# A linear-attention and gated-MLP kernel on one core: a new order of the work, five instead of eight unread products at the start, and three small inputs in fewer packets

## The chip, the cores and the metric

The kernel runs on one core of a Trainium2 chip. The core has a matrix engine (TensorE, PE in the profile, with PEld for its weight loads), three engines for elementwise work (VectorE, DVE; ScalarE, ACT; GpSimd, POOL) and SyncE (SP), which here only issues transfers (DMA). Each engine runs its own instructions strictly in the order in which the program lists them, and waits by semaphores for what another engine or a transfer has to deliver. The metric is the time of one execution on the device in microseconds (us), the median over runs.

## The reference, cut to what matters

Four batches of four heads, sequence 1088, head dimension 32. Attention without softmax: each key and query is turned into 64 products of two 8-wide sketches. Then a gated MLP whose gate mixes along the sequence with a 1088 x 1088 matrix.

```python
def phi(x):
    a = np.einsum('rd,bhsd->bhsr', S1, x)
    b = np.einsum('rd,bhsd->bhsr', S2, x)
    return np.einsum('bhsi,bhsj->bhsij', a, b).reshape(*x.shape[:-1], r * r)
q_p, k_p = (phi(q), phi(k))
kv = np.einsum('bhsf,bhsd->bhfd', k_p, v)
z = np.sum(k_p, axis=2)
num = np.einsum('bhsf,bhfd->bhsd', q_p, kv)
den = np.einsum('bhsf,bhf->bhs', q_p, z)[..., None] + 1e-06
x = num / den                                # heads side by side: (4, 1088, 128)
...
h = np.maximum(x @ w_in, 0.0)                # (4, 1088, 1024)
u, v = (h[..., :d_ff // 2], h[..., d_ff // 2:])
v_n = (v - mu) / np.sqrt(var + 1e-06)        # mean and variance over the last axis
v_s = np.einsum('ts,bsd->btd', w_spatial, v_n) + b_spatial[None, :, None]
return ((u * v_s) @ w_out).astype(np.float32)
```

Some inputs (`S1`, `S2`, `w_in`, `w_out`) arrive as 64-bit floats, and the core turns them into 32-bit ones.

## The kernel before, in words

**Precision.** Large matrix products are made of three: every operand is split into a high half (rounded to the type that TensorE takes at full rate, `F32R`) and a low half, what is left. `high x high`, `high x low` and `low x high` are added up in one bank. So each product needs a cast on ScalarE (the high half) and a subtraction on VectorE or GpSimd (the low half). The spatial weights' halves are `wTh` and `wTl`, those of the normalised v are `vh` and `vl`.

**Stages.** For batch 0 (`attention0`), everything starts at once: the sketch matrices `sk` are loaded and turned from 64 bits to 32 in seven VectorE steps (`from_f64`, L459 to L470). TensorE projects keys and then queries by them in three groups (`project`, L559), ScalarE copies one factor (L564), VectorE multiplies the two into features (L567), TensorE sums keys against values (L606) into `kv`, and VectorE spreads `kv` to the block form `kd0` with a mask (L632). Query features are turned by TensorE with an identity (L655), multiplied with `kd0` (L669), divided on VectorE (L673 to L676), turned again (L683) and split into the halves `xh`, `xl` of x (L687, L688). The second half of the hidden layer, v, is made of 512-column products (L394 to L396), rectified on ScalarE (L771), and normalised with VectorE's statistics (L773 to L800) on VectorE (L809) or ScalarE (L812). Batch 0's v is split per block of 128 rows: L877 on ScalarE, L880 on VectorE (or GpSimd).

`main` then goes over blocks of 128 hidden features (d, four of them) and of output columns (c, three of them): per block nine products groups over the sequence (`spatial`: L940, L942 with the high half of the weights, L949 and L951 with the low half, the last with the bias as two extra rows), the first half of the hidden layer (`hidden`, L932 rectifies it), the gate (L977, then split by L474 and L404), and the output product (`out_mm`, L394 to L396 into a bank `po`). In batch 0 the first column block is done for all four d at once, first all products with the weights' high half, then with the low half. The attention of batch b+1 (`attention`) is woven into batch b's `main`; there the quotient is an elementwise reciprocal of 384 columns on VectorE (L747) and a product (L748), between the sums on TensorE and the 512-column products.

**Loads.** SP issues all transfers in one order, and at most eight are on their way. The first column block of the spatial weights comes in nine slices (`wt00` to `wt80`) into eight buffers (`pl`); a buffer is free again when both halves of its slice are made. The bias goes through a split and back by two transfers into rows of `wTl` (L536).

**What sets the order.** `Order.schedule` is a planner that runs when the program is built. Every operation has a cost written beside it, and a due time: TensorE's work in `main` has due times from `T_MAIN` and `PACE`, the others get theirs backwards from what uses them, shifted by the table `LEADS`. The planner keeps a clock per engine and repeatedly takes, of what could start first (within `SLACK`), the operation with the earliest due time. `FIRST` names loads that go ahead of the others. `AFTER` keeps batch 1's loads behind 35 us of the planner's clock; the built program has no such clock, only the order. Buffers come from pools with a fixed number of tiles, so the order also sets when an operation gets its buffer.

**Unread products.** At the very start TensorE does `N_WARM` products of zeros (L417), and where the planner sees TensorE without work for long enough in the first 50 us it puts further ones in (`fill`, L421; one for each `FILL` ns of the gap). Nobody reads them; they keep TensorE busy. In the profile each such product is two records.

## Time and profile before

| | |
|---|---|
| median of 3 runs (lowest to highest) | 335.91 us (334.52 to 336.27) |
| the profiled execution: its time, its span | 336.3 us, 334.5 us |
| busy in the span: PE, DVE, ACT, POOL | 326.8, 204.3, 157.2, 57.6 us |
| busy share of the 16 transfer engines, 5 to 10 and 10 to 15 us | 0.97, 0.96 |
| HBM read, written | 13.78 MB, 2.23 MB |

The span runs from the first to the last instruction. A row of the order of time gives start and length in us, engine, source line, operation, the tile written and the tiles read, their sizes, and the number of instructions in the row; in brackets stands the idle time just before it and what ended that idle time. Matrix products are pipelined and their ends are modelled, so the lengths of neighbouring rows overlap, and starts are the better measure. Tile names leave out buffer numbers.

### The profile page before, as it was taken

To read this page: it belongs to the slowest core of one execution; us is meant where nothing else is said; L and a number is where in the kernel's file an instruction comes from. 1 tells how busy PE (TensorE), PEld (TensorE's weight loads), DVE (VectorE), ACT (ScalarE), POOL (GpSimd) and SP (SyncE) were. 2 spreads that over 40 slices of the span, in tenths; PEclk is the share of its full clock that TensorE was granted. 3 is DMA by queue.
4 is the path that set the end of the run, shared out by engine and by line. 5 is a ranking of instruction groups with operands and counts; after the bars stand their busy time and mean duration, and the time that the engine had idled before them with its cause. 6 is when DMAs were issued, how large, how long until landed. Compare 5 with 4: busy or idle time off the path is not lost.

```text
span 334.5 us, 6021 instructions
## 1 busy us (share of the span) xinstructions
PE 326.8 (98%) x2308; PEld 314.6 (94%) x2308; DVE 204.3 (61%) x451; ACT 157.2 (47%) x366; POOL 57.6 (17%) x68
## 2 busy tenths in 40 slices
PE   8999999999999999999999999999999999999995
PEld 8977988999999999999999999999999999999994
DVE  3999999253899976679378566728783142121222
ACT  2599675434566762565445625445452242121212
POOL 1000112772423143420032316020000000000000
PEclk9999999999999999999999999999999999999999
DMA  7932267677210266401004173000000001000001
GB/s 225 314 118 69 52 174 222 139 140 164 81 50 21 51 117 153 116 6 43 2 20 77 65 135 62 2 0 0 3 0 2 22 3 44 0 2 0 0 2 67
DMA packets 18196, 23.09 MB, mean 69 GB/s; under 512 B 3064, under 2 KB 17912, under 8 KB 18168
## 3 DMA queue, kind: packets, MB, share of 16 engines
q1 hardware_dynamic: 18168, 22.71, 26.9%
q8 instruction: 18, 0.29, 0.4%
q14 instruction: 10, 0.08, 0.1%
HBM read 13.78 MB, written 2.23 MB: 48 GB/s over the span
## 4 chain that ended last, share of the span: by engine, by line
PE 82%; DVE 7%; DMA 4%; ACT 3%; SPq 1%; issue 1%; DVEq 0%; ACTq 0%
PE sp L940 20%; PE sp L942 17%; PE sp L949 17%; PE sd L394 3%; PE sd L395 3%; PE sd L396 3%; PE po L395 2%; PE pu L394 2%; PE po L394 2%; PE po L396 2%; PE sp L951 2%; PE pu L396 2%; PE pu L395 2%; PE sd L606 2%; DVE wTl L524 2%; DMA v<-in_vA 2%
## 5 line engine op out<-in xcount | busy, mean ns | idle before, releaser
L940 PE MATMUL sp<-wTh,vh 128*128 128x362 f32 (+4 forms) x414 | 135.4, 327 | 0.0
L942 PE MATMUL sp<-wTh,vl 128*128 128x362 f32 (+4 forms) x368 | 119.9, 326 | 0.6 <-DVE vl L880 0.6
L949 PE MATMUL sp<-wTl,vh 128*128 128x362 f32 (+4 forms) x368 | 117.6, 325 | 0.0
L940 PEld LDWEIGHTS sp<-wTh,vh 128*128 128x128 f32 x414 | 77.9, 188 | 1.4 <-ACT vh L877 0.2
L942 PEld LDWEIGHTS sp<-wTh,vl 128*128 128x128 f32 x368 | 69.2, 188 | 1.7 <-DVE vl L880 1.0
L949 PEld LDWEIGHTS sp<-wTl,vh 128*128 128x128 f32 x368 | 69.2, 188 | 0.2
L977 DVE TENSOR_TENSOR u<-sp,u 128x362 f32<-128x362 f32 (+3 forms) x36 | 18.2, 505 | 32.3 <-PE sp L951 27.6
L474 ACT CAST g<-u 128x362 fp32r<-128x362 f32 (+3 forms) x35 | 16.8, 481 | 30.4 <-DVE u L977 30.3
L747 DVE RECIPROCAL c<-c 128x384 f32<-128x384 f32 (+1 forms) x9 | 21.8, 2418 | 14.2 <-ACT c L745 11.5
L773 DVE BATCH_NORM_STATS2 st<-vt 128x6 f32<-128x512 f32 x36 | 24.2, 685 | 6.9 <-ACT vt L771 6.7
L771 ACT ACTIVATE vt<-sd 128x512 f32<-128x512 f32 x36 | 21.3, 600 | 13.1 <-PE sd L396 12.6
L977 DVE TENSOR_TENSOR kp<-sp,kp 128x424 f32<-128x424 f32 x10 | 6.0, 597 | 34.1 <-PE sp L951 34.1
L404 DVE TENSOR_TENSOR g<-u,g 128x362 fp32r<-128x362 f32 (+3 forms) x35 | 20.3, 581 | 8.6 <-ACT g L474 8.1
L716 POOL TENSOR_TENSOR pl<-pl,pl 128x384 f32<-128x384 f32 (+1 forms) x18 | 18.3, 1018 | 35.6 <-DMA pl<-abT 34.3
L407 POOL TENSOR_TENSOR r<-pl,r 128x384 fp32r<-128x384 f32 (+1 forms) x18 | 18.0, 1008 | 37.0 <-ACT r L474 36.9
L407 POOL TENSOR_TENSOR r<-c,r 128x384 fp32r<-128x384 f32 (+1 forms) x9 | 8.9, 993 | 86.9 <-ACT r L474 76.3
L849 ACT CAST vh<-vt 128x384 fp32r<-128x384 f32 x36 | 17.9, 512 | 11.4 <-DVE vt L809 9.0
L932 ACT ACTIVATE u<-pu 128x362 f32<-128x362 f32 (+3 forms) x36 | 16.4, 455 | 14.3 <-PE pu L396 14.3
L851 DVE TENSOR_TENSOR vl<-vt,vh 128x384 fp32r<-128x384 f32 (+1 forms) x36 | 19.4, 549 | 4.7 <-ACT vh L849 4.4
L394 PE MATMUL pu<-xh,wih 128*128 128x362 f32 (+4 forms) x48 | 16.0, 334 | 0.6 <-ACT kp L932 0.6
L809 DVE TENSOR_SCALAR vt<-vt,mv,sm 128x512 f32<-128x512 f32 x32 | 15.8, 537 | 0.0
L396 PE MATMUL pu<-xh,wil 128*128 128x362 f32 (+4 forms) x48 | 15.7, 327 | 0.0
(169 smaller groups left out, 546.7 us busy)
## 6 DMA issues: line engine op xcount, KB each, us to landing
pl<-in_wT SPq DMA_DIRECT2D x18, 166.0 KB, 2.6
v<-in_vA SPq DMA_DIRECT2D x12, 198.0 KB, 2.7
kt<-in_kT SPq DMA_DIRECT2D x12, 192.0 KB, 3.5
pl<-abT SPq DMA_DIRECT2D x12, 192.0 KB, 3.8
pl<-in_wT SPq DMA_DIRECT2D x9, 212.0 KB, 5.9
c<-in_qT SPq DMA_DIRECT2D x9, 192.0 KB, 2.6
pl<-abT SPq DMA_DIRECT2D x24, 72.0 KB, 2.5
pl<-abT SPq DMA_DIRECT2D x6, 160.0 KB, 4.0
```

The source lines that it names most:

```text
L394: nc.tensor.matmul(o, ah, bh, start=start, stop=False)
L395: nc.tensor.matmul(o, ah, bl, start=False, stop=False)
L396: nc.tensor.matmul(o, al, bh, start=False, stop=stop)
L404: return lambda: nc.vector.tensor_tensor(out=o(), in0=a(), in1=bb(), op=ALU.subtract)
L407: return lambda: nc.gpsimd.tensor_tensor(out=o(), in0=a(), in1=bb(), op=ALU.subtract)
L747: op("DVE", 135 + 6.3 * n, lambda x32=x32, n=n: nc.vector.reciprocal(out=x32[:, :n], in_=x32[:, :n]), w=[x32])
L771: op("ACT", c_act(512, True), lambda pv=pv, t=t: nc.scalar.activation(vt[:, t], pv.ap, AF.Relu), r=[pv], w=[(vt, t)])
L773: op("DVE", 690, lambda stats=stats, t=t: nc.vector.bn_stats(out=stats.ap, in_=vt[:, t]), r=[(vt, t)], w=[stats])
L940: nc.tensor.matmul(sp[:, :cw], vh[:, kt], wTh[:, kt, cs], start=(kt == 0), stop=False)
L942: nc.tensor.matmul(sp[:, :cw], vl[:, kt], wTh[:, kt, cs], start=False, stop=False)
L949: nc.tensor.matmul(sp[:, :cw], vh[:, kt], wTl[:, kt, cs], start=False, stop=False)
L977: op("DVE", c_dve(cw), lambda: nc.vector.tensor_tensor(out=u.ap, in0=sp[:, :cw], in1=u.ap, op=ALU.mult), r=[sp], w=[u], lead=LEAD[1])
```

## The change

It does six things.

1. `N_WARM` goes from 8 to 5.
2. The planner multiplies TensorE's costs by `COLD` = 1.25 before 6.8 us of its clock and counts one fill for each 460 ns of a gap there instead of 224. The unread products' own cost goes from 420 to 379 ns.
3. The planner's model of a load changes: a later landing of 1.05 to 1.95 us after issue, and a rate of 0.19 KB/ns before and 0.33 after 7.4 us of its clock, in place of 0.38 with one stop of 1.9 us.
4. The mask (128 rows of 24 bytes) becomes six more columns of the identity, so one transfer brings both; its readers read these columns.
5. The bias is laid out as 17 rows of 64 numbers instead of 68 rows of 16, in its load and in the two transfers into `wTl`, and its tiles come from the pools `abT` and `r`.
6. All tables of the planner are new (`T_MAIN`, `PACE`, `STRETCH`, `FIRST`, `LEADS`, `LEAD`, `SLACK`), so the order of everything is new. `FIRST` names four loads of the second and third column block.

```diff
-N_WARM = 8
+N_WARM = 5
...
-T_MAIN = (36.0, 126.0, 244.0, 299.0)
-PACE = (1.305, 0.8, 1.056, 1.506)
-STRETCH = 1.85
+T_MAIN = (26.0, 113.0, 216.0, 300.0)
+PACE = (1.043, 0.959, 1.6, 1.236)
+STRETCH = 3.08
...
-FIRST = ('wt22', 'wt11', 'wt02', 'qt02', 'wt01')
+FIRST = ('wt01', 'wt42', 'wt21', 'wt22')
...
-LEADS = {'W0': 19500, 'W0.0': -3000, 'W0.1': 18800,
...
+LEADS = {'W0': 4700, 'W0.0': -2000, 'W0.1': -10400,
...
-LEAD = (6500, 3700)
+LEAD = (8600, 700)
...
-SLACK = {'PE': 32, 'ACT': 56, 'DVE': 106, 'POOL': 890, 'SP': 84}
+SLACK = {'PE': 0, 'ACT': 0, 'DVE': 80, 'POOL': 1348, 'SP': 388}
 FILL, FILL_TO, FILL_SPARE = 224, 50.0, 150
+
+COLD_TO, FILL_COLD, COLD = 6800, 460, 1.25
...
-                n = int((s - free[e] - FILL_SPARE) // FILL)
+                n = int((s - free[e] - FILL_SPARE) // (FILL if s > COLD_TO else FILL_COLD))
...
+                cost *= COLD if s < COLD_TO else 1
...
-                dma = max(dma, s + cost + 1950) + o.kb / (0.38 if o.kb > 0 else -0.12)
-
-                if dma > 5000 and not slow:
-                    slow, dma = True, dma + 1900
+
+                late = 1950 if o.kb <= 0 else 1050 if s < 6000 else 1400
+                dma = max(dma, s + cost + late)
+                dma += o.kb / (-0.12 if o.kb <= 0 else 0.19 if dma < 7400 else 0.33)
...
-            kw["due"] = FIRST.index(t.name) - 1e4
+            kw["due"] = FIRST.index(t.name) * 1e5 - 1e8
...
-        op("PE", 420, f4=True, fn=lambda: nc.tensor.matmul(wps[:, :P], z9.ap, z9.ap, start=True, stop=True), r=[z9], w=[wps], due=0)
+        op("PE", 379, f4=True, fn=lambda: nc.tensor.matmul(wps[:, :P], z9.ap, z9.ap, start=True, stop=True), r=[z9], w=[wps], due=0)
...
-    ident = tl(None, "ident_sb", [P, P])
-    load(ident, lambda: ident.ap, idn, 64)
-
-    mask = tl(None, "mask_sb", [P, 6])
-    load(mask, lambda: mask.ap, msk, 2)
+
+
+    ident = tl(None, "ident_sb", [P, P + 6])
+    load(ident, lambda: ident.ap, idn, 70)
...
-        b32 = tl(None, "b32", [68, 16])
-        load(b32, lambda: b32.ap, bsp, 4)
-        bh, bl = tl(None, "bh", [68, 16], F32R), tl(None, "bl", [68, 16], F32R)
-        split(lambda: bh.ap, lambda: bl.ap, lambda: b32.ap, 16, [b32], [bh], [bl])
+        b32 = tl("abT", "b32", [P, 64])
+        load(b32, lambda: b32[:17], bsp, 4)
+        bh, bl = tl("r", "bh", [P, 64], F32R), tl("r", "bl", [P, 64], F32R)
+        split(lambda: bh[:17], lambda: bl[:17], lambda: b32[:17], 64, [b32], [bh], [bl])
...
-            in1=mask[:, 2:].unsqueeze(2).broadcast_to([P, 4, D + 1]), op=ALU.mult,
-        ), r=[kv, mask], w=[kd0])
+            in1=ident[:, P + 2:].unsqueeze(2).broadcast_to([P, 4, D + 1]), op=ALU.mult,
+        ), r=[kv, ident], w=[kd0])
```

Three places show how the order moves. Line numbers of the changed kernel are two or three higher for the same operation. First, TensorE's first instructions: L417 (now L420) and L421 (now L424) are unread, `sk,kt` is a projection of keys and `sk,c` of queries, `v,kp` the sums of keys and values, `ident_sb,kp` a turn of query features. Before:

```order
L417 MATMUL sd_76<-z_67 128x128 x8
L421 MATMUL po_113<-z_67 128x64 x3
L559 MATMUL sd_117<-sk,kt 64x2x32 x6
L559 MATMUL sd_76<-sk,kt 64x2x32 x6
L421 MATMUL po_113<-z_67 128x64 x4
L559 MATMUL sd_117<-sk,kt 64x2x32 x6
L421 MATMUL po_113<-z_67 128x64 x4
L606 MATMUL pu_162<-v,kp_132 64x66 x12
L559 MATMUL sd_76<-sk,c_95 64x2x32 x6
L606 MATMUL pu_162<-v,kp_138 64x66 x12
L606 MATMUL pu_162<-v,kp_151 64x66 x12
L559 MATMUL sd_117<-sk,c_136 64x2x32 x6
```

And now:

```order
L420 MATMUL sd_76<-z_67 128x128 x5
L424 MATMUL po_108<-z_67 128x64 x3
L561 MATMUL sd_112<-sk,kt 64x2x32 x6
L561 MATMUL sd_76<-sk,kt 64x2x32 x6
L424 MATMUL po_108<-z_67 128x64 x3
L561 MATMUL sd_112<-sk,kt 64x2x32 x6
L608 MATMUL pu_148<-v,kp_131 64x66 x12
L561 MATMUL sd_76<-sk,c_88 64x2x32 x6
L424 MATMUL po_108<-z_67 128x64 x4
L608 MATMUL pu_148<-v,kp_137 64x66 x12
L657 MATMUL po_108<-ident_sb,kp_131 128x128 x3
L657 MATMUL po_204<-ident_sb,kp_131 128x128 x3
```

Three products of the first kind and five fills are gone up to the first sums, the first query's turn comes ahead of the third group of sums, and the second and third queries' projections follow those sums. Further on five fills (four before) stand ahead of the first turn of x, and none ahead of the first L669.

Second, VectorE from the first features on: L567 (now L569) are features, of keys three times and then of queries, L460 to L470 (now L463 to L473) the steps that turn `w_in` (`vt`, then `v`) to 32 bits, L676 (now L678) the first quotient. Before:

```order
L567 TENSOR_TENSOR kp_151<-ka_130,sd_117 128x768
L460 TENSOR_SCALAR vt_155<-vt_155 128x512
L462 TENSOR_SCALAR vt_155<-vt_155 128x512
L463 SCALAR_TENSOR_TENSOR vt_155<-vt_89,vt_155 128x512
L567 TENSOR_TENSOR kp_132<-ka_134,sd_76 128x768
L468 TENSOR_SCALAR vt_155<-vt_155 128x512
L632 TENSOR_TENSOR kd_232<-pu_162,mask_sb 128x132
L469 SCALAR_TENSOR_TENSOR vt_155<-vt_89,vt_155 128x512
L567 TENSOR_TENSOR kp_138<-ka_130,sd_117 128x768
L470 TENSOR_TENSOR vt_155<-vt_155 128x512
L567 TENSOR_TENSOR kp_151<-ka_134,sd_76 128x768
L673 TENSOR_SCALAR sm_283<-sp_258 128x12
```

And now, from the third key features to the third query features:

```order
L569 TENSOR_TENSOR kp_163<-ka_129,sd_112 128x768
L569 TENSOR_TENSOR kp_131<-ka_133,sd_76 128x768
L463 TENSOR_SCALAR vt_175<-vt_175 128x512
...
L471 TENSOR_SCALAR vt_175<-vt_175 128x512
L634 TENSOR_TENSOR kd_237<-pu_148,ident_sb 128x132
L472 SCALAR_TENSOR_TENSOR vt_175<-vt_94,vt_175 128x512
L569 TENSOR_TENSOR kp_137<-ka_129,sd_112 128x768
L473 TENSOR_TENSOR vt_175<-vt_175 128x512
L675 TENSOR_SCALAR sm_272<-sp_249 128x12
...
L678 TENSOR_TENSOR c_119<-sp_249,sm_272 128x384
L407 TENSOR_TENSOR wil<-vt_175,wih 128x512
L466 SCALAR_TENSOR_TENSOR v<-kt,v 128x512
L569 TENSOR_TENSOR kp_131<-ka_133,sd_76 128x768
```

The first query features move ahead of the conversion, and the third ones from ahead of the first quotient's steps (L673) to behind the quotient, as does `wil`, the low half of `w_in`, which stood between L673 and L676.

Third, VectorE near the end of batch 0's products with the weights' high half: L524 (now L526) is a low half of spatial weights, L880 (now L882) one of v. Before:

```order
L880 TENSOR_TENSOR vl<-vt_89,vh 128x512
L800 SCALAR_TENSOR_TENSOR sm_333<-mv_484,sm_283 128x3
L524 TENSOR_TENSOR wTl<-pl_240,wTh 64x424
L800 SCALAR_TENSOR_TENSOR sm_333<-sm_333,sm_283 128x3
L524 TENSOR_TENSOR wTl<-pl_216,wTh 128x424
L800 SCALAR_TENSOR_TENSOR sm_283<-sm_333,sm_283 128x3
L524 TENSOR_TENSOR wTl<-pl_218,wTh 128x424
L800 SCALAR_TENSOR_TENSOR sm_381<-mv_484,sm_283 128x3
L524 TENSOR_TENSOR wTl<-pl_185,wTh 128x424
L809 TENSOR_SCALAR vt_155<-vt_155,mv_484,sm_283 128x512 x2
L524 TENSOR_TENSOR wTl<-pl_230,wTh 128x424
L880 TENSOR_TENSOR vl<-vt_155,vh 128x512
```

And now:

```order
L882 TENSOR_TENSOR vl<-vt_94,vh 128x512
L802 SCALAR_TENSOR_TENSOR sm_316<-mv_466,sm_272 128x3
L526 TENSOR_TENSOR wTl<-pl_258,wTh 128x424
L802 SCALAR_TENSOR_TENSOR sm_316<-sm_316,sm_272 128x3
L526 TENSOR_TENSOR wTl<-pl_226,wTh 128x424
L802 SCALAR_TENSOR_TENSOR sm_272<-sm_316,sm_272 128x3
L526 TENSOR_TENSOR wTl<-pl_172,wTh 128x424
L802 SCALAR_TENSOR_TENSOR sm_372<-mv_466,sm_272 128x3
L811 TENSOR_SCALAR vt_175<-vt_175,mv_466,sm_272 128x512 x2
L526 TENSOR_TENSOR wTl<-pl_196,wTh 128x424
L882 TENSOR_TENSOR vl<-vt_175,vh 128x512
```

Counted from the start to the last row shown, VectorE has seven low halves of spatial weights before and five now, and six low halves of v against five; the sixth is GpSimd's first one (L882, a tensor of 128 x 512). The low halves that are no longer here follow later, and so does the ninth slice's, whose load now follows two query loads of batch 1 on SP.

20 lines of the change are left out of this document (10 added, 10 removed).

## Prediction

> **What bounds the kernel now.** I read the busy time of each engine cut into stretches, then that of two source lines alone (L421 and L417, whose products nobody reads), then the order of time at the start, then the later waits. In the stretches the columns are length, then PE, PEld, DVE, ACT and POOL busy (instructions), clock, DMA share, GB/s.
>
> ```profile
> 0.00:5.00 5.00, 3.67 (x17) 3.67 (x18) 1.76 (x10) 1.49 (x2) 1.22 (x8) 1.00 0.57 176
> 15.00:20.00 5.00, 4.33 (x40) 4.19 (x40) 4.33 (x12) 5.00 (x13) 0.00 (x0) 1.00 0.44 148
> 25.00:30.00 5.00, 4.43 (x23) 3.66 (x23) 4.93 (x20) 4.69 (x11) 0.00 (x0) 1.00 0.37 116
> 40.00:45.00 5.00, 4.43 (x24) 3.89 (x23) 4.94 (x11) 4.51 (x12) 0.00 (x0) 1.00 0.63 170
> 55.00:60.00 5.00, 4.34 (x25) 3.77 (x24) 4.10 (x8) 2.51 (x6) 0.91 (x2) 1.00 0.73 203
> 80.00:320.00 240.00, 240.00 (x1595) 233.56 (x1594) 140.24 (x300) 107.05 (x249) 38.28 (x42) 1.00 0.18 40
> 320.00:334.50 14.50, 10.61 (x70) 10.12 (x68) 3.78 (x8) 3.36 (x8) 0.00 (x0) 0.99 0.12 40
> ```
> ```profile
> sum 334.50, PE 5.58 PEld 5.20; mean PE 0.33 PEld 0.31
> ```
> ```profile
> sum 334.50, PE 3.78 PEld 3.49; mean PE 0.22 PEld 0.21
> ```
>
> From 60 us on TensorE never rests: 240.00 of 240.00 between 80 and 320, and 3.89 idle in the last stretch, whose instructions the change leaves in their order. What can move is TensorE's lost time in the first 60 us: 5.58 in L421, 3.78 in L417 (the two sum rows), 1.33 before the first product, and idle 0.67, 0.57, 0.57 and 0.66 in four stretches, together 13.2. VectorE is the second limit: 4.93 of 5.00 busy at 25 us, 4.94 still at 40.
>
> **Step 1, the start.**
>
> ```profile
> 1.33 3.78 PE L417 MATMUL sd<-z 128*128 128x128 f32 x16 [1.33 <-DVE z L413]
> 4.91 1.38 PE L421 MATMUL po<-z 128*128 128x64 f32 x6
> 6.22 1.02 PE L559 MATMUL sd<-sk,kt 128*64 128x64 f32 x24
> 7.16 1.10 PE L421 MATMUL po<-z 128*128 128x64 f32 x8
> 8.21 0.57 PE L559 MATMUL sd<-sk,kt 128*64 128x64 f32 x12
> 8.71 1.10 PE L421 MATMUL po<-z 128*128 128x64 f32 x8
> 9.74 0.92 PE L606 MATMUL pu<-v,kp 128*64 128x66 f32 x24
> 10.50 0.52 PE L559 MATMUL sd<-sk,c 128*64 128x64 f32 x12
> ```
> ```profile
> 4.86 0.23 DVE L470 TENSOR_TENSOR sk<-sk 128x64 f32<-128x64 f32 x1
> ...
> 6.93 0.59 ACT L564 COPY ka<-sd 128x96 f32<-128x96 f32 x2 [4.70 <-PE sd L559]
> ...
> 7.20 2.85 DVE L567 TENSOR_TENSOR kp<-ka,sd 128x768 f32<-128x768 f32 x3 [2.12 <-ACT ka L564]
> ```
>
> The clock column reads 1.00 from the first stretch, yet durations show a slow start: six records of L421 take 1.31 us from 4.91 to 6.22 (0.22 each), eight take 1.03 from 8.71 to 9.74 (0.13 each), a factor 1.7. Eight unread products end at 4.91, 0.45 each; five end at 3.57, and three fills later, at 4.88, TensorE is free. The sketch matrices `sk` are ready at 5.09 (4.86 + 0.23). So the first projection starts near 5.15, not 6.22: 1.07 earlier. It now runs at the slow pace: 0.8 instead of 0.47 (two took 0.94). I take 0.75 of gain for ScalarE's copy and for VectorE's first feature product, 7.20 to 6.45; the bounds are 1.07 (pace irrelevant) and 0.4 (both projections slow).
>
> **Step 2, VectorE's new order up to the first hidden product.**
>
> ```profile
> 12.69 0.29 DVE L632 TENSOR_TENSOR kd<-pu,mask_sb 128x132 f32<-128x132 f32 x1
> ...
> 14.89 0.68 ACT L457 ACTIVATE v<-kt 128x512 f32<-128x512 f32 x1 [0.53 <-DMA pl<-in_wT]
> ...
> 16.65 0.69 DVE L404 TENSOR_TENSOR wil<-vt,wih 128x512 fp32r<-128x512 f32 x1 [0.67 <-ACT wih L474]
> ...
> 17.68 0.55 DVE L676 TENSOR_TENSOR c<-sp,sm 128x384 f32<-128x384 f32 x1
> ...
> 18.28 0.55 PE L683 MATMUL sp<-ident_sb,c 128*128 128x128 f32 x3 [0.67 <-DVE c L676]
> ```
> ```profile
> 20.25 0.48 PE L394 MATMUL sd<-wih,xh 128*128 128x512 f32 x1
> ```
>
> The three key products now end at 9.3 (6.45 + 2.85). The first query product, formerly behind three conversion steps, stands right behind them and waits: third projection at 7.4 (its bank is freed by the first product) to 7.9, twelve products of L606 (0.76) to 8.66, the query's projection (0.5, as from 8.21 to 8.71) and copy (0.3, half of L564's 0.59) to 9.5. VectorE loses 0.2. Next, `kd`: four fills, the second L606 group, six transposes (0.8) and the third group put the sums at 12.7, where they were (12.69): the 0.75 is spent there. But the third query product (0.9) and `wil` with its 0.67 wait no longer stand ahead of the first quotient L676: two projections and the sums (1.34) after 12.5 end at 14.85, and L676 comes at about 16.1, 1.5 earlier. The second half of `w_in` is issued when the third projection is done, so it comes about 0.75 earlier and ScalarE's 14.89 becomes 14.2 to 14.9; later would cost VectorE up to 0.4. TensorE has to run six transposes (0.8) and five fills (1.3) first: the turn of x moves from 18.28 to 17.0. Behind L676 VectorE does `wil`, a conversion step and the third query product (2.1 by before's rows), so x's low half and then L394 come at 19.55, not 20.25. **Step 2 leaves 0.7.** Bounds: 0, since `kd` alone gains nothing, and 1.3.
>
> **Step 3, the later waits.** After 20 us TensorE idles 1.8 (0.57, 0.57, 0.66 by the stretches).
>
> ```profile
> 27.95 0.46 PE L394 MATMUL pu<-xh,wih 128*128 128x424 f32 x1 [0.34 <-ACT kp L932]
> ```
> ```profile
> 43.01 0.46 PE L942 MATMUL sp<-wTh,vl 128*128 128x424 f32 x1 [0.57 <-DVE vl L880]
> ...
> 56.79 0.46 PE L394 MATMUL po<-xh,woh 128*128 128x424 f32 x1 [0.49 <-ACT xh L474]
> ```
> ```profile
> 30.95 0.60 DVE vl L880
> ...
> 39.26 0.51 DVE wTl L524
> ```
>
> The last two rows are the chain's pieces for one low half of v and of the spatial weights. Ahead of the low half that 43.01 waits for, VectorE now does two L524 fewer (7 to 5, 1.0) and one L880 fewer (0.6, moved to GpSimd), and one conversion step more (0.4): 1.2 less. I take that 0.57 as gone, the others as staying. The output product of 56.79 stands behind nine products of the next block and more, but these need a bank that VectorE frees; so the wait may only change its name. Bounds: 1.8 gone, or one more wait of their size, 0.6 lost. **Sum for the start: 0.7 + 0.6 = 1.3.**
>
> **Step 4, the smaller edits.** Mask with identity and the bias in 17 rows: no engine's wait in the trace ends with one of these loads, so 0; the cover is their lead over L632 and the transposes near 12.7, and uncovered the mask's own packets cost at most the 0.4 of one load's issue.
>
> ```profile
> 0.74 0.40 SPq L401 DMA_DIRECT2D kt<-in_kT  x1
> ```
> ```profile
> pl<-in_wT SPq DMA_DIRECT2D x18, 166.0 KB, 2.6
> ...
> kt<-in_kT SPq DMA_DIRECT2D x12, 192.0 KB, 3.5
> ...
> pl<-in_wT SPq DMA_DIRECT2D x9, 212.0 KB, 5.9
> ...
> mask_sb<-in_msk SPq DMA_DIRECT2D x1, 3.0 KB, 4.8
> ```
>
> The last rows give KB and time to landing. The first four loads keep their places; kT, issued at 0.74, lands 3.5 later, before 5.15. The first query's load moves ahead of the 512 KB of `w_in` and is needed at 8.66. The ninth spatial slice is now loaded near 35 us, when VectorE frees a buffer, past two of the next batch's query loads on SP's queue: it lands 2.6 to 5.9 later, and its products follow those of 43 us. All 0; uncovered, each costs its lateness in full.
>
> **Step 5, the steady part.** The new due times move the later attention stages. In batch 2, between the last sums product of group 0 and the first hidden product that needs its quotient, stand 12 groups of products instead of 14, 1.0 less; in batch 3, 12 instead of 15, 1.5 less.
>
> ```profile
> 139.56 0.56 DVE L404 TENSOR_TENSOR xl<-c,xh 128x384 fp32r<-128x384 f32 x1 [0.19 <-ACT xh L474]
> ```
> ```profile
> 140.69 0.39 PE L396 MATMUL sd<-wih,xl 128*128 128x512 f32 x1
> ```
> ```profile
> 208.26 1.36 DVE L404 TENSOR_TENSOR xl<-c,xh 128x384 fp32r<-128x384 f32 x1
> ```
> ```profile
> 210.07 0.39 PE L396 MATMUL sd<-wih,xl 128*128 128x512 f32 x1
> ```
>
> The low half is ready at 140.12, its user starts at 140.69: 0.57 to spare, against 1.0 taken away; in batch 3, 209.62 and 210.07: 0.45 against 1.5. If the quotients take as long as now, TensorE waits 0.4 and 1.05. The 1.36 is a stretched copy of the 0.56 above, so the chain can shrink by 0.8. I take 0.3 of a range 0 to 1.45.
>
> **The sum.** -0.7 - 0.6 + 0.3 = -1.0. The profiled execution took 336.3 (span 334.5, 1.8 around it) and becomes 335.3; the median of the runs shown is 335.91, 0.4 less, so I say **334.9**.
>
> **Rivals.** *(a) All early waits go.* VectorE has work taken off before 43 us; then 0.7 + 1.8 = 2.5 less and no new wait, 333.4. For it: the 1.2 above. Against: 4.9 busy of 5.00, so any new wait there comes back. *(b) The steady part pays.* Batch 2 and 3 wait 1.45 at the quotients; with the start's gain cut to 0.7 the time is 336.7, slower than before. It decides once those waits exceed what the start gained. For it: spare times of 0.45 and 0.57, smaller than the cuts. Against: with such small spares, before shows no wait there. *(c) The slow pace lasts longer.* Fewer unread products, and a rest of 0.2 at 4.9, may keep TensorE slow. If the slow time (1.33 to about 6.3) lasts as long again, projections and L606 groups of about 3 us cost 0.7 more each: +2.0, 336.9. Against: the unread products still fill it from 1.33 to 4.88.
> [...] *(d) No gain arrives*: VectorE, with the same total to do before the products of 43 us, sets their time as now, and the 0.75 ends at `kd`: 335.9. For it: `kd` at 12.7. Against: the work moved behind L676.
>
> **Chances.** Forecast (gain 0.4 to 1.7) 0.45, (a) 0.25, (b) 0.12, (c) 0.06, (d) 0.12. For 8 in 10 the range leaves out the far ends of (a) and (b): 333.2 to 336.7. About 0.5% (1.7 us) is what a measurement can tell from no change: faster 0.27 ((a) and the forecast's edge), slower 0.06 (both (b) and (c) at their worst), same 0.67.
>
> **What would show it.** Right: L559 first at about 5.15, L567 at 6.45, L632 still near 12.7, L676's successor at 16 to 16.3, the first 512-column hidden product near 19.5, no TensorE wait for L882 at 41 to 43. Wrong: fills still 0.22 each after 6.5 us; `kd` after 13; a TensorE gap of over 0.3 before the 512-column products near 135 to 155 or 200 to 212; a wait for a bank at 50 to 55 as long as the old 0.66.

## The result and the profile after

The changed kernel takes 340.73 us (median of 6 runs, 339.17 to 343.67), the kernel before, timed beside it, 335.18 us (6 runs, 334.52 to 336.27). The ratio is 1.0161, with a 95% interval of 1.0135 to 1.0188: slower by 1.6%, outside the range of the prediction (333.2 to 336.7). Its runs also lie 4.5 us apart, those of before 1.8. The profiled execution took 340.9 us with a span of 339.1, so 4.6 us of span are to be found.

First the same stretches as before the change: length, then PE, PEld, DVE, ACT and POOL busy (instructions), clock, DMA share, GB/s.

```profile
25.00:30.00 5.00, 4.42 (x24) 3.45 (x22) 5.00 (x22) 3.91 (x10) 0.00 (x0) 1.00 0.29 88
40.00:45.00 5.00, 4.31 (x21) 3.60 (x21) 4.94 (x12) 3.38 (x7) 0.25 (x1) 1.00 0.67 195
55.00:60.00 5.00, 4.64 (x27) 4.04 (x26) 3.54 (x6) 4.12 (x11) 2.93 (x3) 1.00 0.83 282
80.00:320.00 240.00, 239.25 (x1582) 231.84 (x1581) 140.03 (x300) 107.19 (x249) 38.69 (x42) 1.00 0.18 40
```

The idle time hardly grew: 0.58, 0.69 and 0.36 in the three early stretches (0.57, 0.57 and 0.66 before), 0.75 between 80 and 320 us (none before). But between 80 and 320 us TensorE started 1582 instructions where it had started 1595, in a stretch in which it was called busy nearly throughout. The order has changed, so the stretch no longer holds quite the same instructions, and the count alone settles nothing. But 0.75 us of idle time is worth only four or five of these products, and products that follow each other more slowly would not show in a table of busy and idle time. So the distances from start to start have to be compared.

TensorE's start after the change, in order of time (start, length, engine, line, operation, tiles, shapes, count):

```profile
1.33 2.50 PE L420 MATMUL sd<-z 128*128 128x128 f32 x10 [1.33 <-DVE z L416]
3.63 1.38 PE L424 MATMUL po<-z 128*128 128x64 f32 x6
5.18 1.55 PE L561 MATMUL sd<-sk,kt 128*64 128x64 f32 x24 [0.18 <-DVE sk L473]
6.66 1.54 PE L424 MATMUL po<-z 128*128 128x64 f32 x6
8.14 0.91 PE L561 MATMUL sd<-sk,kt 128*64 128x64 f32 x12
8.83 1.53 PE L608 MATMUL pu<-v,kp 128*64 128x66 f32 x24
10.15 0.81 PE L561 MATMUL sd<-sk,c 128*64 128x64 f32 x12
10.90 1.10 PE L424 MATMUL po<-z 128*128 128x64 f32 x8
...
18.32 0.55 PE L685 MATMUL sp<-ident_sb,c 128*128 128x128 f32 x3
...
21.01 0.48 PE L397 MATMUL sd<-wih,xh 128*128 128x512 f32 x1
```

The first projection starts at 5.18, as predicted, but TensorE keeps its slow pace: the six records of fills from 6.66 to 8.14 take 0.25 each, a sums group (L608) of 1.32 from start to start where it was 0.76. Only the fills of 10.90 run at 0.13. Before, the slow pace ended near 6.3. The first 512-column product comes at 21.01; it was at 20.25.

VectorE at the start, and TensorE's later waits:

```profile
6.41 1.82 DVE L569 TENSOR_TENSOR kp<-ka,sd 128x768 f32<-128x768 f32 x2 [1.28 <-ACT ka L566]
9.36 0.95 DVE L569 TENSOR_TENSOR kp<-ka,sd 128x768 f32<-128x768 f32 x1 [1.13 <-ACT ka L566]
11.29 0.95 DVE L569 TENSOR_TENSOR kp<-ka,sd 128x768 f32<-128x768 f32 x1 [0.97 <-ACT ka L566]
...
14.56 0.29 DVE L634 TENSOR_TENSOR kd<-pu,ident_sb 128x132 f32<-128x132 f32 x1 [0.33 <-DMA pl<-in_wT]
...
17.71 0.55 DVE L678 TENSOR_TENSOR c<-sp,sm 128x384 f32<-128x384 f32 x1
```
```profile
43.11 0.47 PE L942 MATMUL sp<-wTh,vh 128*128 128x424 f32 x1 [0.24 <-ACT vh L879]
...
44.02 0.46 PE L944 MATMUL sp<-wTh,vl 128*128 128x424 f32 x1 [0.45 <-DVE vl L882]
...
125.56 0.44 PE L398 MATMUL po<-g,woh 128*128 128x364 f32 x1 [0.67 <-DVE g L407]
```

The first features come 0.8 earlier (6.41), the third key product waits 1.13 for its slow projection, `kd` comes at 14.56 instead of 12.69. The wait of 43.01 is not gone, it is two waits now, and there is a new one of 0.67 at 125.56.

**The pace.** One row of the costliest groups (shapes apart; the number behind the comma is the mean length in ns) for the 128 products with the weights' low half that are 362 columns wide, before and after:

```profile
L949 PE MATMUL sp<-wTl,vh 128*128 128x362 f32 x128 | 41.7, 326 | 0.0
```
```profile
L951 PE MATMUL sp<-wTl,vh 128*128 128x362 f32 x128 | 42.1, 329 | 0.0
```

Three ns look like nothing; over all large products they are the largest single piece of the loss. To size it I take, for each product of 240 or more columns, the time to the start of the next one less the fastest that its size shows (107 ns for 240 columns, 143 for 320, 147 for 332, 161 for 362, 162 for 364, 171 for 384, 187 for 424, 227 for 512), leave out steps more than 25 ns longer, which are waits or changes of kind, and add up. This **pace sum** is 6.9 us before and 9.0 after; 2.0 of the 2.1 between them lie in the spatial products.

So the 4.6 us of span divide as follows: 0.8 until the first 512-column product; 2.1 of pace; 0.7 at the wait of 125.56; and 1.0 in smaller gaps, most of it at 42 to 46 us, where TensorE waits for v's halves.

### The profile page after: what moved, and what is told of

It is laid out like the page before. It is cut to its first block, busy times and chain, and to the rows that moved or that the text cites. A ratio compares the mean times of both kernels' runs of the same rounds, so it can differ in the third digit from the quotient of the medians.

```text
span 339.1 us, 6003 instructions
## 1 busy us (share of the span) xinstructions
PE 330.9 (98%) x2300; PEld 316.6 (93%) x2300; DVE 204.6 (60%) x450; ACT 157.1 (46%) x366; POOL 60.4 (18%) x69
## 4 chain that ended last, share of the span: by engine, by line
PE 75%; DVE 15%; DMA 4%; ACT 3%; issue 1%; SPq 1%; DVEq 0%
PE sp L942 18%; PE sp L951 16%; PE sp L944 16%; PE sd L397 3%; PE sd L399 3%; PE sd L398 3%; PE po L398 2%; DMA pl<-in_wT 2%; PE po L399 2%; PE po L397 2%; PE sp L953 2%; PE sd L608 2%; PE pu L397 2%; PE pu L398 2%; PE pu L399 2%; DMA v<-in_vA 2%
## 5 line engine op out<-in xcount | busy, mean ns | idle before, releaser
L951 PE MATMUL sp<-wTl,vh 128*128 128x362 f32 (+4 forms) x368 | 119.0, 328 | 0.0
L979 DVE TENSOR_TENSOR u<-sp,u 128x362 f32<-128x362 f32 (+3 forms) x36 | 18.2, 505 | 36.3 <-PE sp L953 34.3
L979 DVE TENSOR_TENSOR kp<-sp,kp 128x424 f32<-128x424 f32 x10 | 6.0, 598 | 35.1 <-PE sp L953 35.1
L407 DVE TENSOR_TENSOR g<-u,g 128x362 fp32r<-128x362 f32 (+3 forms) x35 | 20.8, 594 | 9.6 <-ACT g L477 9.2
L718 POOL TENSOR_TENSOR pl<-pl,pl 128x384 f32<-128x384 f32 (+1 forms) x18 | 19.1, 1060 | 35.7 <-DMA pl<-abT 33.4
L853 DVE TENSOR_TENSOR vl<-vt,vh 128x384 fp32r<-128x384 f32 (+1 forms) x36 | 18.6, 536 | 1.9 <-ACT vh L851 1.4
L410 POOL TENSOR_TENSOR r<-c,r 128x384 fp32r<-128x384 f32 (+1 forms) x9 | 9.6, 1067 | 46.2 <-ACT r L477 43.9
L811 DVE TENSOR_SCALAR vt<-vt,mv,sm 128x512 f32<-128x512 f32 x32 | 16.9, 571 | 0.0
```

The source lines that it names most:

```text
L407: return lambda: nc.vector.tensor_tensor(out=o(), in0=a(), in1=bb(), op=ALU.subtract)
L410: return lambda: nc.gpsimd.tensor_tensor(out=o(), in0=a(), in1=bb(), op=ALU.subtract)
L951: nc.tensor.matmul(sp[:, :cw], vh[:, kt], wTl[:, kt, cs], start=False, stop=False)
L979: op("DVE", c_dve(cw), lambda: nc.vector.tensor_tensor(out=u.ap, in0=sp[:, :cw], in1=u.ap, op=ALU.mult), r=[sp], w=[u], lead=LEAD[1])
```

## Experiments on the pace: the addresses

On-chip memory is handed out in the order in which the program first uses each tile. So a new order, which touches no address on purpose, moves nearly every tile. The first two experiments exchange the addresses and nothing else: every engine's instructions stay the same, waits included.

```diff
+LAYOUT = [('kt', [128, 3, 384], 0), ('eps', [128, 1], 0), ('z9', [128, 128], 0), ...]
...
+    laid = {n: const.tile(shape, F32R if r else F32, name=n) for n, shape, r in LAYOUT}
     def place(t):
         if t.tag is None:
-            return const.tile(t.shape, t.dt, name=t.name)
+            return laid[t.name][:t.shape[0]]
```

**The changed kernel with the addresses of before.**

> The changed kernel, instruction for instruction, with every tile of on-chip memory at the address it had in the kernel before (the tiles are made in a listed order at the start). In the two traces the large steady products start 1.3 ns further apart after the change than before, some 2.6 us over about 1,960 of them, with no wait shown. Theory A (addresses): their pace hangs on where the operands lie; it falls back to that of before, the time to about 338.1 us (340.7 - 2.6). Rival B (order, or chance from run to run): the address does nothing, about 340.7 us. The low first clock and the later waits stay under both: the slow pace still ends near 10.9 us, the first 512-column product is still near 21.0 us.

Measured: 339.68 us (8 runs, 337.01 to 342.19), the kernel before 335.69 beside it; ratio 1.0104 (1.0071 to 1.0138), against 1.0161 (1.0135 to 1.0188) for the change as it is: the intervals just touch. The pace sum is 7.0 us.

**The kernel before with the addresses of the change.**

> The kernel before, instruction for instruction, with every tile at the address it has in the changed kernel. Theory A (addresses): about 2.6 us slower than before, 337.8 us, with the start, the waits at 28, 43 and 57 us and all else of the order as before. Rival B (order or chance): 335.2 us, no change.

Measured: 337.14 us (10 runs, 335.98 to 337.40) against 335.69; ratio 1.0036 (1.0022 to 1.0050). The pace sum is 9.0 us. The same row of the groups, of the first and of the second:

```profile
L952 PE MATMUL sp<-wTl,vh 128*128 128x362 f32 x128 | 41.7, 326 | 0.0
```
```profile
L950 PE MATMUL sp<-wTl,vh 128*128 128x362 f32 x128 | 42.1, 329 | 0.0
```

The 326 and 329 have changed places with the addresses. Theory A holds, the rival falls: the pace of the products is a matter of where their operands lie. By time the addresses are worth 1.45 us in the order of before, by these two traces 2.1. The addresses don't settle everything, though. Two later runs of the kernel before, with fewer unread products but the same order and addresses behind them, have pace sums of 7.4 us in place of 6.9. The first 424 columns of batch 0 make the difference; here are two rows of TensorE's order of time from the kernel before, then two from the run with five unread products:

```profile
38.01 0.35 PE L940 MATMUL po<-wTh,vh 128*128 128x424 f32 x1
...
39.88 0.35 PE L940 MATMUL sp<-wTh,vh 128*128 128x424 f32 x1
```
```profile
38.00 0.36 PE L949 MATMUL po<-wTh,vl 128*128 128x424 f32 x1
...
39.97 0.36 PE L949 MATMUL sp<-wTh,vl 128*128 128x424 f32 x1
```

Ten steps take 1.87 us in the first (187 ns each) and 1.97 in the second (197). So by the traces the addresses are worth 1.5 to 2.1 us.

**Which addresses: products alone.** Three kernels of nothing but products, then a padded one.

```diff
+    for n in NS:
+        for s in range(0, 32, 2):
+            go([(s, W0)], n, 12)
```

> Products of zeros alone, nothing else running, most of the computation left out: groups of twelve products of 240, 332, 362, 364, 424 and 512 columns, the moving operand starting at each multiple of 8 bytes modulo 128, the stationary one at 96 modulo 128; then groups of three in turn with two starts of the moving and two of the stationary operand, as the spatial products have them. Theory A (the address alone sets the pace): start to start 187 ns for 424 columns from 32 modulo 128 and near 195 ns from 64; 161 ns for 362 columns from 80 and 165 or more from 120; a second start of either operand in turn lengthens the fast ones by 4 to 8 ns. If all starts give one pace per size, the address matters only beside the other engines' traffic.

The pace differs between starts with nothing else running: twelve equal products of 332 columns follow at 146 ns from a start of 32 modulo 128 and at 156 from 24, of 362 columns at 160 from 8 and 170 from 64. So other engines' traffic isn't needed. But 424 columns from 32 ran at 193, not at 187, and 362 from 80 at 167, not at 161: the start modulo 128 alone is not the rule. The next kernel has the real strides:

> Only the spatial products, of zeros, in their real order and with the real strides (high x high, low x high, high x low over nine blocks), nothing else running, all else of the computation left out: every cut of columns that the kernel uses, with the weights' halves and v's halves starting at 0, 32, 64 and 96 modulo 128, the two halves alike or as in the changed kernel (weights 32 and 0, v 96 and 32). Theory A (addresses, without other engines' traffic): with 32, 32 and 96, 96 as before the first 424 columns run at 187 ns and the second 424 at 195; with 32, 0 and 96, 32 as after the change both run at 191 to 195, and some starts run every cut at its fast pace. Rival (the pace comes from other engines' accesses, which the address only shifts): no such difference between starts, as for 424 columns from 32 in the groups of equal products, which ran at 193.

None of its 240 groups was at the fast pace throughout, whatever the starts; their means lie 2.3 to 9.9 ns above it. Here the weights' two halves lay 128 apart modulo 256, in the kernel before they lie at the same start modulo 256. So the third sets starts modulo 256:

```diff
+        for dv, dt in ((32, 0), (16, 0), (0, 0), (48, 0), (32, 32), (16, 56)):
+            for x in range(0, 64, 8):
+                x2, y2 = (x + dt) % 64, (y + dv) % 64
```

> The spatial products alone again, of zeros, nothing else computed, now with the operands' starts set modulo 256: the weights' high half at 0 to 224 in steps of 32, v's high half at 96, v's low half 128, 64, 0 or 192 beyond it, the weights' low half 0, 128 or 224 beyond the high one. In the kernel before (weights 32 and 32, v 96 and 224 modulo 256) the first 424, the middle 362 and the last 332 columns run at their fast pace, in the run with starts alike modulo 128 only, none did. Theory A1 (the starts modulo 256 set it): with weights at 32 and 32 and v at 96 and 224 these three cuts run at 187, 161 and 147 ns, and near 193, 166 and 152 at most other starts. Rival A2 (larger distances or the banks of memory set it): no fast cut here either.

Rows of TensorE's order of time for the first 424 columns, from this kernel: a group with the starts of the kernel before, then the next group, with the weights 32 further.

```profile
40.81 0.35 PE L46 MATMUL b<-th,vl 128*128 128x424 f32 x1
...
43.24 0.35 PE L47 MATMUL b<-tl,vh 128*128 128x424 f32 x1
...
43.62 0.36 PE L46 MATMUL b<-th,vl 128*128 128x424 f32 x1
...
46.14 0.36 PE L47 MATMUL b<-tl,vh 128*128 128x424 f32 x1
```

Thirteen steps take 2.43 us (187 ns each) in the first and 2.52 (194) in the second. Theory A1 is borne out here: with the starts of before, the first 424, the middle 362 and the last 332 columns run at 187, 160 and 147. Of the 64 groups with v's halves 128 apart modulo 256 and the weights' halves alike, 9 have a median at the fast pace, with v's halves at the same start 6, and of the 256 other groups none, 192 of them with v's halves 64 or 192 apart. The changed kernel has v's halves 64 apart and the weights' halves 96; this pair of distances was not among the groups.

**A changed kernel with 192 bytes of padding.** It brings the four tiles of the spatial products back to their starts of before, modulo 256. The tiles behind them shift along with the padding, so some others (`woh`, `wol`, most of `g`) come back as well; but the products that read those hold only about 0.1 us of the 2.1.

```diff
+    ('pad0', [128, 8], 0), ('wTl', [128, 9, 1088], 1), ('pl7', [128, 424], 0),
+    ('pad1', [128, 24], 0), ('wTh', [128, 9, 1088], 1), ...
+    ('pad2', [128, 16], 0), ('vl', [128, 8, 4, 128], 1), ...
```

> The changed kernel with eight unread products and 32, 96 and 64 bytes left free ahead of the weights' low half, the weights' high half and v's low half, so that these start at 32, 32 and 224 modulo 256 (v's high half falls to 96), as in the kernel before; every other tile stays where the change put it, but for that shift. Theory A1 (the starts of these four tiles modulo 256 set the pace): pace and time as with all addresses of before, about 2.1 us of product time less than with eight products alone, 337.3 to 338.0 us. If other tiles matter too, 339.5 us as with eight products alone.

Measured: 338.28 us (4 runs, 337.96 to 338.62), before 335.57; ratio 1.0074 (1.0049 to 1.0098), where eight products without padding have 1.0113 (1.0086 to 1.0140; below). The intervals overlap, so the traces carry this reading: the pace sum is 7.1 us where it was 9.0, and the row reads 325:

```profile
L959 PE MATMUL sp<-wTl,vh 128*128 128x362 f32 x128 | 41.6, 325 | 0.0
```

A last kernel of products asked for the rule, and whether a better start exists:

> The spatial products alone once more, of zeros, nothing else computed: the weights' halves alike modulo 256, v's low half 128 beyond its high half (or 0 beyond), now every start of v's high half modulo 256 in steps of 32 against every start of the weights. If the starts of weights and v act together (only their distance counts), the fast cuts move along with v's start. If each has to lie right by itself, the weights at 32 are fast at one or two starts of v alone. From it: the pair of starts with the least time over all cuts, which for the kernel before (weights 32, v 96) is 3.8 us above the fast pace everywhere by the run before; a pair with 2 us or less would make a kernel below 334.5 us.

The distance counts: with v's halves 128 apart, the first 424 columns are fast at all 8 starts of v when the weights start 64 beyond v's high half modulo 256, both 362 cuts when it is 96, the second 424 and the last 332 when it is 160. At 192, the distance of the kernel before, the last 332 were fast at 8 of 8 starts, the first 424 and the middle 362 at 1 of 8 each; in the kernel before these run fast. At the very starts of before (weights 32, v's high half 96) this kernel ran the first 424 columns at 193 and the middle 362 at 163, the one before it at 187 and 160. So at this distance two paces are possible, as the rows further up show for the kernel itself, and what decides between them stays open. The least sum over six cuts was 1.6 us (weights 0, v 64, again at 192 apart), against 3.8 at the starts of before in this run; as the kernel before already has its three cuts fast at the same distance, I made no kernel of it.

## Experiments on the start: the unread products

The planner's order stays; only the number of products at the very start differs, inside the first of them.

```diff
+    done = []
+    def warm():
+        done.append(0)
+        for _ in range(6 - N_WARM + 1 if len(done) == 1 else 1):
+            nc.tensor.matmul(wps[:, :P], z9.ap, z9.ap, start=True, stop=True)
```

> The changed kernel with one unread product more at the very start (six, 0.43 us of TensorE), the order otherwise untouched. After the change TensorE rests 0.18 us before the first projection at 5.18 and its products run at the slow pace until 10.9 us instead of 6.3 us. Theory C (a rest inside the first 6.3 us keeps the clock low): the six fill the rest, first projection near 5.4, slow pace over by about 6.5 us, first 512-column product near 20.0 instead of 21.0, time about 1 us less, 339.7. Rival D (what counts is how much unread work stands ahead, as with eight): still slow until near 10.9 us and the time 340.7 to 341.1.

> The changed kernel with eight unread products as before, the order otherwise untouched: first projection near 6.3 us. Under theory C and rival D alike the slow pace ends near 6.3 us and the first 512-column product comes near 20.3 us as before the change; time 0.7 us less than the changed kernel, 340.0 us. If the slow pace still lasts until 10.9 us, neither the rest nor the number of unread products sets it.

Measured: six give 339.73 us (4 runs, 339.24 to 341.67; ratio 1.0124, 1.0087 to 1.0161), eight 339.53 (4 runs, 339.27 to 340.57; ratio 1.0113, 1.0086 to 1.0140), beside 335.69 for before. First with six, then with eight:

```profile
5.37 1.55 PE L568 MATMUL sd<-sk,kt 128*64 128x64 f32 x24
6.85 0.88 PE L431 MATMUL po<-z 128*128 128x64 f32 x6
...
19.33 0.48 PE L397 MATMUL sd<-wih,xh 128*128 128x512 f32 x1
```
```profile
6.22 1.29 PE L568 MATMUL sd<-sk,kt 128*64 128x64 f32 x24
7.44 0.88 PE L431 MATMUL po<-z 128*128 128x64 f32 x6
```

Both are at full pace by the fills of 6.85 and 7.44 (0.15 each). So the number of unread products, not the order, held the changed kernel at the slow pace until 10.9. Eight instead of five are worth about 0.5% by these ratios, with intervals that touch. How long the slow pace lasts with five varies: the changed kernel with the addresses of before was at it longer still in its profiled execution, the slowest of its eight (six records of transposes at 0.25 each, the projections at full pace):

```profile
14.31 1.54 PE L658 MATMUL po<-ident_sb,kp 128*128 128x128 f32 x6
...
16.86 0.86 PE L562 MATMUL sd<-sk,c 128*64 128x64 f32 x24
```

Its eight times spread over 5.2 us; with eight unread products and the same addresses (below) ten spread over 1.7. The kernel before with five, in turn:

```diff
+        if len(done) > 3:
             nc.tensor.matmul(wps[:, :P], z9.ap, z9.ap, start=True, stop=True)
```

> The kernel before with five unread products instead of eight, its order untouched. If too little dense work at the start keeps the clock low: a short rest before the first projection near 5.1 us, slow pace until 10 us or later in most executions, first 512-column product at 21 us or later, a time of 336.5 to 338 us and runs that lie several us apart. If five are enough in this order: first 512-column product near 19.2 us and 335.0 us.

```profile
3.63 1.31 PE L428 MATMUL po<-z 128*128 128x64 f32 x6
5.24 0.92 PE L566 MATMUL sd<-sk,kt 128*64 128x64 f32 x24 [0.30 <-DVE sk L477]
```

Measured: 337.52 us, 10 runs in two heaps: 334.54, 335.17, 335.29 and 335.56, one at 336.79, and five at 338.25 to 339.08; before 336.56 beside it, ratio 1.0019 (0.9981 to 1.0057). In the profiled execution (336.79) the projections run at full pace from 5.24 on, 0.30 of rest ahead of them notwithstanding. That start is lost again behind it. The first turn of x waits for the quotient:

```profile
18.68 0.55 PE L690 MATMUL sp<-ident_sb,c 128*128 128x128 f32 x3 [1.79 <-DVE c L683]
```

On VectorE the quotient stands behind `wil`, which waits 1.79 us for ScalarE's `wih`, and ScalarE has waited 1.03 us just ahead of it for a load of spatial weights. The first 512-column product comes at 20.65, later than the 20.25 of before. So both readings of the expectation were too simple: with five the times fall into two heaps, and a full pace from 5 us on is no gain when a load comes late. The lower heap is 1 to 2 us below the median of before, as Step 1 of the prediction wanted it (before's own lowest here is 335.34); the upper one is 1.7 to 2.5 above it. The one trace lies between the heaps, so what parts them is not shown; a longer slow pace, as in the changed kernel, is likely.

> The kernel before with six unread products instead of eight, its order untouched; TensorE then has no rest ahead of the first projection near 5.4 us (with five it rested 0.30). If a rest is what keeps the clock low in half of the runs with five: all runs near each other as with eight, first 512-column product between 18.5 and 20 us, 334.8 to 335.5 us, up to 0.8 below before. If what counts is the length of the dense start: runs that lie 3 us apart as with five, and a median of 336 to 338.

Measured: 335.65 us (12 runs, 334.68 to 339.30) against 335.57; ratio 1.0006 (0.9982 to 1.0030). Ten of the twelve lie within 334.7 and 336.6, two at 337.6 and 339.3. Six are nearly always enough in this order, and gain nothing at the median. Whether a rest or the density of the work decides how long the slow pace lasts stays open. Six leave no rest, yet two runs were late; neither has a trace, and one of them (337.63) also has a lower mean granted clock than the others, 0.992 against 0.997 to 1.0.

## Experiments on the order

**The changed kernel with both undone**, the addresses of before and eight unread products:

> The changed kernel with both undone, the addresses of before and eight unread products; its order, packets and loads stay. If the two causes add up: 340.7 - 2.2 (pace, by the traces of the two kernels with exchanged addresses) - 1.2 (unread products, as measured) = 337.3 us, and the 1.8 us that are left over the kernel before belong to the order itself, with the first waits of TensorE after 21 us as in the changed kernel. If it comes to 335.5 us, the order costs nothing; if it stays at 339.5 us or above, the addresses do nothing for the time although they change the pace.

Measured: 338.05 us (10 runs, 336.99 to 338.68) against 336.56, the ratio 1.0016 with 0.9981 to 1.0052: the medians lie 1.5 us apart, but the interval includes a ratio of 1, no change, so the time leaves open what the order costs. The traces say more. The pace sum is 7.1 us. From the first 512-column product to the start of the last product of all it takes 312.5 us, before 310.1: 2.4 us, of which the pace is 0.3. The rest belongs to the order. One piece of it can be taken out. VectorE of the changed kernel ahead of the wait of 125.56:

```profile
122.79 0.49 DVE L860 TENSOR_TENSOR vh<-vt,vh 64x128 fp32r<-64x128 f32 x2
123.31 0.54 DVE L979 TENSOR_TENSOR u<-sp,u 128x364 f32<-128x364 f32 x1
124.41 1.09 DVE L407 TENSOR_TENSOR g<-u,g 128x364 fp32r<-128x364 f32 x1 [0.56 <-ACT g L477]
```

The gate L979 stands behind steps that split v for the blocks to come, and TensorE's output product needs its low half L407. Four of these steps go behind it:

```diff
+    late = [x for x in order if not isinstance(x, Fill) and x.name in ("vh11:4", "vh12:4", "vh13:4", "vl11:3")]
+    order = [x for x in order if x not in late]
+    low = next(i for i, x in enumerate(order) if not isinstance(x, Fill) and x.name == "gl100:1")
+    order[low + 1:low + 1] = late
```

> The changed kernel with the addresses of before and eight unread products, and one step of its order moved: on VectorE four steps that split the second to fourth block of batch 1's v (0.3 to 1.1 us each) now stand behind the gate's product and low half of the first block instead of ahead. In the changed kernel TensorE waits 0.67 us at 125.6 us for that low half. If that wait is VectorE's order: it goes, and the time is 0.6 to 0.7 us below the same kernel without this step (338.05 beside 336.56 for the kernel before), so about 0.8 us above before. If the gate is late for another reason or the moved steps are missed next, TensorE waits as long at 125 to 132 us and the time stays.

```profile
121.00 0.54 DVE L987 TENSOR_TENSOR u<-sp,u 128x364 f32<-128x364 f32 x1 [0.30 <-PE sp L961]
122.10 1.31 DVE L408 TENSOR_TENSOR g<-u,g 128x364 fp32r<-128x364 f32 x1 [0.56 <-ACT g L485]
123.44 0.99 DVE L868 TENSOR_TENSOR vh<-vt,vh 64x128 fp32r<-64x128 f32 x1
```
```profile
123.11 0.33 PE L398 MATMUL po<-g,woh 128*128 128x364 f32 x1
123.47 0.44 PE L399 MATMUL po<-g,woh 128*128 128x364 f32 x1
```

Measured: 337.48 us (4 runs, 337.42 to 338.40) against 335.57; ratio 1.0059 (1.0037 to 1.0081). The listed wait is gone, 0.36 from start to start instead of 1.01, and no new one stands behind it; from the first 512-column product on it takes 312.0 us instead of 312.5. The times don't show this gain: by the ratio to the kernel before, which was 336.56 beside the one run and 335.57 beside the other, this version is no faster than the one without the moved gate. Nor is the wait the order's alone: with eight unread products and the changed kernel's addresses it was 0.14, in the padded kernel 0.25. The other 2.0 us to the kernel before lie, as far as the profile shows, in smaller waits of this order: 0.7 more than before at 41 to 45 us for v's halves, some 0.3 near 97 to 100 us, 0.2 each at 36 and 123 us, the rest smaller still. I didn't test them one by one, so their causes stay open. No version beat the kernel before.

## Why the prediction was wrong, by its steps

**Step 1** foresaw the start of the first projection (5.15, measured 5.18) and of the first features (6.45, measured 6.41). What failed is the sentence that the first projection runs at the slow pace and the work after it as before. It took the end of the slow pace, 6.3, as fixed by time. In the changed kernel it ended at 10.9. That is rival (c), to which I gave 0.06 and 336.9 us. Its place and mechanism were right, its price of 2.0 about right (1.2 us by the medians with eight and five products, 1.7 beside the kernel before of each). Its weight was far too small. I put it down because "the unread products still fill it from 1.33 to 4.88": 3.55 us of dense work, which was enough in one of the three traces with five products (full pace from 5.24).

The traces show when the pace changed. The kernel before and the changed one each have a record of the granted clock that reads 1.0; it begins at 6.46 us in the kernel before and at 10.79 in the changed one, and lasts 327.68 us in both. By the spacing, the first group at full pace throughout starts between 4.89 and 7.60 us in all profiled executions with six or eight products, and with five at 5.24, 10.90 and 16.86. What ends the slow pace, and how much dense work that takes, they do not show.

**Step 2** failed with it: `kd` at 14.56 (foreseen 12.7), L678 at 17.71 (16.1), the turn of x at 18.32 (17.0), the first 512-column product at 21.01 (19.55). The start's 0.7 of gain became 0.8 of loss. Where full pace came about as early as before, the forecast of the start came about: in the changed kernel with six unread products (full pace from 6.85) the turn of x starts at 16.63 and the first 512-column product at 19.33, 0.9 ahead of before. How much of that the order brings is open. In two executions full pace came early, among the fills behind eight unread products; first the order of before (with the addresses of the change), then that of the change (with the moved gate):

```profile
4.89 0.78 PE L422 MATMUL po<-z 128*128 128x64 f32 x6
...
18.94 0.48 PE L395 MATMUL sd<-wih,xh 128*128 128x512 f32 x1
```
```profile
4.91 0.99 PE L432 MATMUL po<-z 128*128 128x64 f32 x6
...
19.40 0.48 PE L398 MATMUL sd<-wih,xh 128*128 128x512 f32 x1
```

The fills end 0.2 earlier in the first, and the product comes 0.5 earlier: the change's order loses. With six products each it is the other way round, 19.33 for the change's order against 19.64 for that of before, whose first turn of x waited 1.04 us for the quotient. With eight, and the first projection at 6.22 in both, it is 20.13 against 20.25.

**Step 3** took 0.57 of the wait of 43.01 as gone, since VectorE has 1.2 less to do ahead. The wait stayed, 0.24 for ScalarE's high half and 0.45 for VectorE's low half, 0.69 together. The late start is not the reason: with the moved gate the first 512-column product came at 19.40, and the two waits were 0.38 and 0.46. The term that failed is the low half that moved to GpSimd, which I counted as 0.6 less for VectorE. While GpSimd works at it, one of VectorE's normalisations takes 1.60 us, where the same one took 0.53 before. GpSimd and VectorE of the changed kernel, then VectorE before:

```profile
34.02 1.29 POOL L882 TENSOR_TENSOR vl<-vt,vh 128x512 fp32r<-128x512 f32 x1 [31.66 <-ACT vh L879]
```
```profile
33.99 1.60 DVE L811 TENSOR_SCALAR vt<-vt,mv,sm 128x512 f32<-128x512 f32 x1
```
```profile
33.50 0.53 DVE L809 TENSOR_SCALAR vt<-vt,mv,sm 128x512 f32<-128x512 f32 x1
```

It is 1.61 in two other executions of this order, again beside GpSimd's step. That costs 1.07 of the 1.2; no run takes GpSimd's step away, so the cause is read from the two times alone. VectorE is as full as before (4.94 of 5.00), and the idle time of the three stretches is 1.6, it was 1.8: next to nothing, where I had 0.6.

**Step 4** set the packets to nothing, and no wait ends with them. But it looked only at when data arrives. The order in which tiles are first used sets their addresses, and no step of the sum, and no rival, had that: 2.1 us by the trace of the change, 1.45 by time in the order of before.

**Step 5** looked for the cost of the steady part at the quotients of batches 2 and 3. None shows there: 20.00 of 20.00 busy in each stretch from 140 to 320. The cost came at a place that I had not looked at, the first gate of batch 1 (0.67), and in small waits of batches 0 and 1. All in all the order costs 1.7 us behind the start by the two profiles (2.1 with both other causes undone), and between 1.0 and 2.5 over all seven profiled executions of this order, mostly above the 1.45 of my range for this step. So rival (b)'s end was about right in size, and its place wrong.

So three costs of the same sign, of which I had weighed one at 0.06, one at 0.12 and one not at all.

## What to carry to other kernels

Unread products at the very start pay only if there are enough of them: with five instead of eight in the kernel before, half of the executions came 3 us later than the best ones, so time such a change in many runs before its median is believed. Work that is moved to another engine is not free: look at what the two engines do to each other's steps (here 1.60 us instead of 0.53 beside GpSimd's step, the cause read from these times alone). When a change of order moves a steady stretch without any wait, compare the time from start to start of equal instructions and the addresses of their operands; here 192 bytes of padding undid 2 us. And a busy share of 100% doesn't mean that the work goes on at the same pace: TensorE was busy 20.00 of 20.00 us in each stretch from 140 to 320 in both kernels, and the products of 362 columns with the weights' low half took 326 ns on average before and 329 after.

## What the hardware did that I had not expected

- The time from one large product to the next hangs on where its operands start, modulo 256 bytes, relative to each other: 187 or 194 ns for 424 columns, 160 or 165 for 362, with the same instructions and no other engine at work.

  The first 424 columns took 187 ns with the weights 64 beyond v's high half and 195 with 96; how this distance sets the time, no run here shows.
- At a distance of 64 the first 424 columns were fast at 8 of 8 starts, at 192 at 1 of 8; there two paces are possible: the first 424 columns of batch 0 ran at 187 ns in the kernel before, and at 197 with the same order and addresses behind five unread products.
- One VectorE step of 512 columns took 1.60 us instead of 0.53 while GpSimd worked at a step of its own.
- The clock column reads 1.00 from the first stretch on while the products' spacing shows the slow pace up to 10.9 us in the changed kernel. Its trace has no clock record ahead of 10.79, and the column counts time without a record as full clock.
- With five unread products the same program's times lie 4.5 us apart (334.54 to 339.08 in one order, 339.17 to 343.67 in the other).
